# A scan feeding a two-layer network: one tile per weight load, and masks spread over the steps

## The chip, the cores and the metric

The kernel runs on one core of one Trainium2 chip. The metric is the time of one execution on the device in microseconds. The kernel before takes 139.41 us (median of three runs, 139.23 to 139.72). The profiled execution took 139.26 us, of which the profile covers a span of 137.5 us.

A core has five engines that run at the same time and wait for each other through semaphores: TensorE (PE, matrix products; PEld is its weight load), VectorE (DVE), ScalarE (ACT), GpSimd (POOL) and SyncE (SP, which here only issues transfers). Matrix products are written to PSUM, eight banks of 128 partitions by 512 fp32 values; the other operands lie in SBUF.

## The reference, cut to what matters

A recurrence with decay over the sequence (4 batches, 8 heads, 768 positions, 32 values and 16 states for each head), in chunks of 32, and then a network with a squared ReLU on the 3072 tokens:

```python
for c in range(nc):                       # chunks of the sequence
    cum = np.cumsum(la, axis=-1)          # la: log of the decays a
    L = np.exp(cum[:, :, :, None] - cum[:, :, None, :]) * causal
    CB = np.einsum('bhin,bhjn->bhij', Cc, Bc)
    y_intra = np.einsum('bhij,bhjd->bhid', CB * L, xc)
    y_inter = np.einsum('bhin,bhnd->bhid', Cc, state) * np.exp(cum)[..., None]
    y[:, :, sl] = y_intra + y_inter
    state = decay_full * state + sum_j(B_j x_j decay_from_j)
# [3072, 256] @ [256, 2048] -> relu, squared -> @ [2048, 256]
h = np.maximum(y_tokens @ w_in, 0.0)
out = h * h @ w_out
```

All inputs and the output are fp32.

## The kernel before

The work is cut into 12 units of 256 tokens (one batch, a third of the sequence). A unit has two chunks of 128 tokens; token `2t + r` of a unit lies at place t, half r. For each unit the kernel

- loads C, B and x, and scales C by the running product P of the decays and x by 1/P (`ph_prep`), so that no exponentials are needed,
- transposes C and B (`ph_tr`), on TensorE for units 0 to 3 and by the transfer engines after that,
- multiplies C and B into PSUM banks 0 to 3 (`ph_mt`) and masks the result into SBUF as bf16 (`ph_mask`, VectorE),
- adds up, in two other banks, y (masked products with x, and C with the state S), and the new state's sum U of both chunks (`ph_yu`), and copies y to `T`, which is what the network reads,
- makes S from U (`ph_s`): z = U + S before on VectorE, S = z times the decay on GpSimd, and a copy spread over the heads.

The network runs in steps of 256 hidden units, eight for each unit of tokens: `mm1` (four products into one bank, then ReLU on ScalarE), `square` on VectorE one step later, `mm2` four steps later. The work on the next units is hung into these steps. PSUM banks 4, 5 and 6 go round for `mm1`, y and U; bank 7 holds the output.

The loads of the weights, their casts to bf16, and the masks:

```python
BLOCKS = [(0, 2), (2, 4), (4, 8), (8, 12), (12, 16)]   # 128 hidden units each
w_in_b = wpool.tile([128, 2, 2048], BF16, name="w_in_b")
w_out_b = wpool.tile([128, 16, 256], BF16, name="w_out_b")
w_in_f = stage.tile([128, 2, 2048], FP32, name="w_in_f")
w_out_f = stage.tile([128, 16, 256], FP32, name="w_out_f")

def load_w(i, eng=None):
    f0, f1 = BLOCKS[i]
    (eng or nc.sync).dma_start(out=w_in_f[:, :, f0 * 128:f1 * 128], in_=...)
    (eng or nc.sync).dma_start(out=w_out_f[:, f0:f1, :], in_=...)

def cast_w(fp):
    f = 2 * fp
    f0, f1 = next(x for x in BLOCKS if x[0] <= f < x[1])
    nc.scalar.copy(out=_fap(w_in_b, f * 128, [[2048, 2], [128, 2], [1, 128]]),
                   in_=_fap(w_in_f, f0 * 128 + f - f0, [[2048, 2], [1, 2], [f1 - f0, 128]]))
    nc.gpsimd.tensor_copy(out=w_out_b[:, f:f + 2, :], in_=w_out_f[:, f:f + 2, :])

def ph_mask(k, q0, q1):        # banks q0 to q1 - 1
    nc.vector.tensor_tensor(out=live[k]["mts"][:, q0:q1]..., in0=pp[:, q0:q1, :],
                            in1=<the mask>, op=ALU.mult)
```

The order of the first part, and of the steps:

```python
ph_load(0, ...); load_w(0); load_w(1); ph_load(1)
load_w(2); load_w(3); ph_load(2); load_w(4); ph_load(3)
# ... decays, ph_prep and ph_tr of unit 0 ...
ph_mt(0)
ph_mask(0, 0, 1)
ph_yu(u=0)
ph_s(0, 0)
ph_s(0, 1)
for q in range(1, 4):
    ph_mask(0, q, q + 1)
cast_w(0)
cast_w(1)
ph_yu(y=0, late=True)          # y of unit 0, then the copy to T

for fp in range(2, 8):
    at(fp - 2, cast_w, fp)     # hung into steps 0 to 5
# unit 1: prep at step 1, ph_tr at 2, U and ph_mt at 3, ph_s and masks at 4 and 5, y at 7
# unit 2: prep at 4, ph_tr at 8, U and ph_mt at 9, ph_s and masks at 10 and 11
# unit 3: prep at 9, ph_tr at 10
for k in range(2, NU):         # from unit 2 on: the region of unit k
    s0 = 8 * k - 4
    at(s0, ph_yu, y=k, u=k + 1)
    at(s0, ph_mt, k + 1)
    for i in range(2):
        at(s0 + 1 + i, ph_s, k + 1, i)
        at(s0 + 1 + i, ph_mask, k + 1, 2 * i, 2 * i + 2)
```

Of the kernel before, what the change touches and what calls it, by code (L numbers as in the profile page):

```python
# [10 lines left out]
FP32 = mybir.dt.float32  # L11
BF16 = mybir.dt.bfloat16
AF = mybir.ActivationFunctionType
# [17 lines left out]
def kernel(  # L31
# [104 lines left out]
    def load_w(i, eng=None):  # L136
        f0, f1 = BLOCKS[i]
        (eng or nc.sync).dma_start(  # L138
            out=w_in_f[:, :, f0 * 128:f1 * 128],
            in_=_dap(moe_w_in, f0 * 128, [[2048, 128], [128 * 2048, 2], [1, (f1 - f0) * 128]]))  # L140
        (eng or nc.sync).dma_start(
            out=w_out_f[:, f0:f1, :],
            in_=moe_w_out[f0 * 128:f1 * 128, :].rearrange("(p f) d -> p f d", p=128))

    def cast_w(fp):
        f = 2 * fp
        f0, f1 = next(x for x in BLOCKS if x[0] <= f < x[1])
        nc.scalar.copy(out=_fap(w_in_b, f * 128, [[2048, 2], [128, 2], [1, 128]]),  # L148
                       in_=_fap(w_in_f, f0 * 128 + f - f0, [[2048, 2], [1, 2], [f1 - f0, 128]]))
        nc.gpsimd.tensor_copy(out=w_out_b[:, f:f + 2, :], in_=w_out_f[:, f:f + 2, :])  # L150

    live = {}

# [33 lines left out]
    def ph_tr(k):  # L187
        v = live.setdefault(k, {})
        bct = big.tile([128, 2, 3, 128], BF16, tag="bct", name=f"bct{k}")
        v["bct"] = bct  # L190
        if k >= NPE:
            nc.sync.dma_start_transpose(out=bct.rearrange("p r w t -> p (r w) t"),
                                        in_=jt[k % 3].rearrange("p r w t -> p (r w t)"))
            return
# [28 lines left out]
    def ph_yu(y=None, u=None, late=False):  # L223

        h = two_banks()
        begun = set()

        def mm(i, quads, dst, w, v, pos):
            need = [(i, q) for q in quads if (i, q) not in begun]
            begun.update(need)  # L230
            assert len(need) in (0, len(quads))
            nc.tensor.matmul(dst, w, v, start=bool(need), stop=False, skip_group_check=True,  # L232
                             **({} if pos is None else {"tile_position": pos}))

        def from_state():
            for i in range(2):
                S_i = live[y]["S"][i]
                if S_i is None:
                    continue
                for g in range(2):  # L240
                    mm(i, range(4), pp[:, h[i], g * 128:(g + 1) * 128], S_i[:, g * 128:(g + 1) * 128],
                       _fap(live[y]["bct"], 128 + g * 128 + i * 64, [[384, 2], [1, 64]]), None)

        if y is not None:
            v = live[y]
            if not late:
                from_state()
            for g in range(2):
                for r in range(2):
                    for i in range(2):  # L250
                        for q in range(4):
                            hd = 4 * g + q
                            mm(i, [q], pp[32 * q:32 * q + 32, h[i], g * 128:(g + 1) * 128],
                               v["xs"][64 * i:64 * i + 64, r, hd * 32:hd * 32 + 32],
                               v["mts"][64 * i:64 * i + 64, q, r, g, :], (64 * i, 32 * q))
# [11 lines left out]
        if y is not None:  # L267
            if late:
                from_state()
            T[y] = tpool.tile([128, 2, 2, 2, 64], BF16, tag="T", name=f"T{y}")  # L270
            nc.scalar.copy(out=_fap(T[y], 0, [[64, 2], [128, 4], [1, 64]]),  # L271
                           in_=_fap(pp, h[0] * 512, [[512, 2], [64, 4], [1, 64]]))
            live.pop(y)

    def ph_s(k, i):

        b, j = UNITS[k]
        v = live[k]
# [9 lines left out]
        if prev is None:  # L288
            nc.vector.tensor_scalar(out=S_c, in0=U, scalar1=ptot, scalar2=None, op0=ALU.mult)  # L289
        else:  # L290
            z = spool.tile([128, 64], FP32, tag="z", name=f"z{k}_{i}")
            nc.vector.tensor_tensor(out=z, in0=U, in1=prev, op=ALU.add)  # L292
            nc.gpsimd.tensor_scalar(out=S_c, in0=z, scalar1=ptot, scalar2=None, op0=ALU.mult)  # L293
        S_d = spool.tile([128, 256], BF16, tag=f"Sd{b}{i}", name=f"Sd{k}_{i}")
        nc.gpsimd.tensor_tensor(  # L295
            out=_fap(S_d, 0, [[128, 2], [32, 4], [1, 32]]), in0=_fap(S_c, 0, [[32, 2], [0, 4], [1, 32]]),
# [6 lines left out]
    def mm1(blk, fp):  # L303
        h = bank()
        for i in range(2):
            f = 2 * fp + i
            for g in range(2):
                nc.tensor.matmul(pp[:, h, i * 256:(i + 1) * 256], w_in_b[:, g, f * 128:(f + 1) * 128],  # L308
                                 T[blk][:, g].rearrange("p r u t -> p (r u t)"),
                                 start=(g == 0), stop=(g == 1), skip_group_check=True)  # L310
# [10 lines left out]
    def mm2(blk, fp):  # L321
        h2 = h2s.pop((blk, fp))
        for i in range(2):
            f = 2 * fp + i
            for r in range(2):
                nc.tensor.matmul(pp[:, 7, r * 256:(r + 1) * 256], h2[:, i, r * 128:(r + 1) * 128],  # L326
                                 w_out_b[:, f, :], start=(f == 0 and r == 0), stop=(f == 15),
                                 skip_group_check=True)
        if fp == 7:
            b, j = UNITS[blk]  # L330
# [4 lines left out]
    with tc.manual_schedule():  # L335
# [8 lines left out]
        ph_load(1)  # L344
        load_w(2)
        load_w(3)
        ph_load(2)
        load_w(4)
        ph_load(3)

        nc.vector.memset(zer, 0.0)
        nc.vector.memset(jt[0], 0.0)
        for i in range(1, 3):
            nc.gpsimd.memset(jt[i], 0.0)
        nc.vector.tensor_scalar(out=a_cl, in0=a_nat, scalar1=1e-6, scalar2=1.0, op0=ALU.max, op1=ALU.min)
        for u in range(2):
            nc.vector.tensor_tensor_scan(out=cp_r[:, u * 128:(u + 1) * 128], data0=a_cl[:, u * 128:(u + 1) * 128],
# [3 lines left out]
        for r in range(2):  # L361
            nc.tensor.transpose(ptr[:, r, :], _fap(cp_r, r, [[2, 128]]), eye_f)
        nc.scalar.copy(out=P_sb, in_=ptr)
        prep_b(0, nc.scalar)
        prep_c(0, nc.vector)
        nc.vector.reciprocal(out=_fap(Pinv, 0, [[96, 2], [3, 32]]), in_=_fap(P_sb, 0, [[96, 2], [3, 32]]))
# [4 lines left out]
        hp = bank()  # L371
        pps = pp[:, hp, 0:24].rearrange("p (u c) -> p u c", u=2)
# [12 lines left out]

        steps = [(b, f) for b in range(NU) for f in range(8)]
        todo = {}
# [11 lines left out]
        at(3, ph_mt, 1)  # L399
        at(4, ph_s, 1, 0)  # L400
        at(4, ph_s, 1, 1)
        at(4, ph_mask, 1, 0, 2)
        at(5, ph_mask, 1, 2, 4)
# [10 lines left out]
        for k in range(2, NU):  # L414
# [54 lines left out]
```

## Time and profile before

| engine | busy, us | share of the span | instructions |
|---|---|---|---|
| TensorE, products | 108.0 | 79% | 1572 |
| TensorE, weight loads | 89.3 | 65% | 1572 |
| VectorE | 84.0 | 61% | 158 |
| ScalarE | 78.7 | 57% | 133 |
| GpSimd | 55.3 | 40% | 104 |

The profile has several views. The page gives the busy share of each engine in 40 equal slices of the span, as digits in tenths. Its groups are instructions of one line, engine and operation: after the bar stand the busy time in us and the mean of one in ns, then how long the engine stood idle just before them, and what ended that wait. The timeline is in order of time: start, duration, engine, line, operation, output<-input, count, and in brackets the idle time before and its releaser. An engine with q behind its name is its instruction queue, which issues transfers; the duration there is the issue and not the transfer. The list of waits sums who waited for whom. The chain of waits goes back from the last instruction to what released it, step by step.

The chain of waits of the kernel before gives TensorE 61% of the span, VectorE and ScalarE 9% each, the queue that issues transfers 9% and the transfers 7%. The largest lines in it are the two products of the network, with 28% and 25%.

### The profile page before, as it was taken

Reading aid. Unit: us, or ns where it says so; the run is one execution under the profiler, and the core shown is the slowest. Engines: PE = TensorE matmul, PEld = TensorE weight load, DVE = VectorE, ACT = ScalarE, POOL = GpSimd, SP = SyncE. Lnnn points to the kernel's source line nnn. Section 1 sums busy time; section 2 is a strip of 40 time slices with the busy share of each in tenths; the row PEclk is TensorE's granted clock in tenths of the full one; section 3 lists DMA queues with packets and bytes.
Section 4 is the critical chain, followed back from the end, with each engine's and each line's share of the span. In section 5 each row is a group of like instructions: output and inputs, shape, how many; then the busy total and the mean of one; then the engine's idle time right before and its main releaser. Section 6 shows DMA issues by size and latency. Waiting matters only on the chain.

```text
span 137.5 us, 3855 instructions
## 1 busy us (share of the span) xinstructions
PE 108.0 (79%) x1572; PEld 89.3 (65%) x1572; DVE 84.0 (61%) x158; ACT 78.7 (57%) x133; POOL 55.3 (40%) x104
## 2 busy tenths in 40 slices
PE   0164000569999898998998989999999999999990
PEld 0141000437877786877887868888888878888770
DVE  1558000158799976869869778696786839534430
ACT  2200000997836567575675756767667676686640
POOL 4037190109966663916828349190542003000000
PEclk9999999999999999999999999999999999999999
DMA  5999999996001679539929599187902802010101
GB/s 93 235 303 205 368 243 303 214 150 131 0 5 51 127 120 114 94 82 141 150 90 90 111 120 164 58 97 146 119 19 89 49 2 81 2 76 5 76 0 76
DMA packets 48034, 15.81 MB, mean 115 GB/s; under 512 B 44240, under 2 KB 45072, under 8 KB 48016
## 3 DMA queue, kind: packets, MB, share of 16 engines
q1 hardware_dynamic: 46720, 15.18, 59.3%
q10 hardware_dynamic: 1296, 0.39, 1.7%
q8 instruction: 12, 0.20, 0.6%
q14 instruction: 6, 0.05, 0.1%
HBM read 10.84 MB, written 3.15 MB: 102 GB/s over the span
## 4 chain that ended last, share of the span: by engine, by line
PE 61%; DVE 9%; ACT 9%; SPq 9%; DMA 7%; issue 2%; ACTq 1%; DVEq 0%
PE pp L308 28%; PE pp L326 25%; SPq L130 7%; PE pp L232 6%; DVE mts L219 5%; DMA cb<-const_b 4%; ACT hb L312 3%; DMA w_in_f<-in_moe_w_in_dram 3%; ACT T L271 3%; ACT w_in_b L148 2%; DVE h L318 2%; PE pp L210 2%; DVE z L292 1%; ACT osb L332 1%; SPq L138 1%
## 5 line engine op out<-in xcount | busy, mean ns | idle before, releaser
L312 ACT ACTIVATE hb<-pp 128x512 bf16<-128x512 f32 x96 | 57.4, 598 | 29.7 <-PE pp L308 29.6
L308 PE MATMUL pp<-T,w_in_b 128*128 128x256 bf16 x384 | 60.0, 282 | 14.7 <-ACT T L271 12.4
L318 DVE TENSOR_TENSOR h<-hb 128x512 bf16<-128x512 bf16 x96 | 47.7, 515 | 33.5 <-ACT hb L312 32.6
L326 PE MATMUL pp<-w_out_b,h 128*128 128x256 bf16 x384 | 57.6, 275 | 0.3 <-ACT osb L332 0.3
L308 PEld LDWEIGHTS <-w_in_b 128*128 128x128 bf16 x384 | 37.4, 101 | 23.1 <-ACT w_in_b L148 11.6
L326 PEld LDWEIGHTS <-h 128*128 128x128 bf16 x384 | 37.9, 99 | 5.2 <-issue 0.5
L219 DVE TENSOR_TENSOR mts<-pp,cb 128x1024 bf16<-128x1024 f32 (+1 forms) x26 | 29.2, 1131 | 0.8 <-PE pp L210 0.8
L293 POOL TENSOR_SCALAR Sc<-z,Ptot 128x64 f32<-128x64 f32 x16 | 7.1, 443 | 35.5 <-DVE z L292 35.5
L148 ACT CAST w_in_b<-w_in_f 128x512 bf16<-128x512 f32 x8 | 7.8, 990 | 15.4 <-DMA w_in_f<-in_moe_w_in_dram 15.4
L295 POOL TENSOR_TENSOR Sd<-Sc,cb 128x256 bf16<-128x256 f32 x20 | 12.2, 612 | 10.2 <-DVE Sc L289 8.9
L174 POOL TENSOR_TENSOR xs<-x_nat,Pinv 128x512 bf16<-128x512 f32 x12 | 13.2, 1102 | 5.2 <-DMA x_nat<-in_x_dram 5.2
L157 POOL TENSOR_TENSOR jt<-C_nat,P_sb 128x128 bf16<-128x128 f32 x20 | 10.7, 554 | 0.0
L271 ACT CAST T<-pp 128x512 bf16<-128x512 f32 x12 | 7.0, 584 | 2.9 <-PE pp L232 2.6
L292 DVE TENSOR_TENSOR z<-pp,Sc 128x64 f32<-128x64 f32 x16 | 3.5, 221 | 7.7 <-ACT T L271 7.4
L150 POOL CAST w_out_b<-w_out_f 128x512 bf16<-128x512 f32 x8 | 4.8, 619 | 8.4 <-DMA w_out_f<-in_moe_w_out_dram 8.4
L232 PE MATMUL pp<-mts,xs 64*32 64x128 bf16 x384 | 6.2, 225 | 2.4 <-DVE mts L219 1.7
L332 ACT COPY osb<-pp 128x512 f32<-128x512 f32 x12 | 7.0, 581 | 1.6 <-PE pp L326 1.6
L169 POOL CAST jt<-B_nat 128x128 bf16<-128x128 f32 x22 | 7.2, 353 | 0.0
L232 PEld LDWEIGHTS <-xs 64*32 64x32 bf16 x384 | 3.5, 93 | 4.3 <-issue 3.2
L210 PE MATMUL pp<-bct 32*64 32x256 bf16 x192 | 5.6, 303 | 0.3 <-DVE bct L200 0.3
L232 PE MATMUL pp<-bct,Sd 128*128 128x128 bf16 x40 | 5.0, 223 | 0.5
L232 PE MATMUL pp<-xs,jt 64*32 64x64 bf16 x160 | 4.0, 203 | 1.3 <-ACT hb L312 1.1
(28 smaller groups left out, 27.3 us busy)
## 6 DMA issues: line engine op xcount, KB each, us to landing
x_nat<-in_x_dram SPq DMA_DIRECT2D x12, 256.0 KB, 4.7
out_dram<-osb SPq DMA_DIRECT2D x12, 256.0 KB, 3.9
C_nat<-in_C_dram SPq DMA_DIRECT2D x12, 128.0 KB, 4.1
w_in_f<-in_moe_w_in_dram SPq DMA_DIRECT2D x3, 512.0 KB, 5.4
w_out_f<-in_moe_w_out_dram SPq DMA_DIRECT2D x3, 512.0 KB, 6.1
B_nat<-in_B_dram SPq DMA_DIRECT2D x11, 128.0 KB, 4.3
w_in_f<-in_moe_w_in_dram SPq DMA_DIRECT2D x2, 256.0 KB, 5.6
w_out_f<-in_moe_w_out_dram SPq DMA_DIRECT2D x2, 256.0 KB, 5.6
```

The lines of the kernel that those rows point to most:

```text
L130: (eng or nc.sync).dma_start(out=dst, in_=_dap(src, (b * NH * S + j * 256) * w, [[2 * w, 128], [S * w, NH], [1, 2 * w]]))
L148: nc.scalar.copy(out=_fap(w_in_b, f * 128, [[2048, 2], [128, 2], [1, 128]]), in_=_fap(w_in_f, f0 * 128 + f - f0, [[2048, 2], [1, 2], [f1 - ...
L157: eng.tensor_tensor(out=_fap(jt[k % 3], 128 + 144 * g, [[384, 2], [32, 4], [1, 16]]), in0=_fap(loaded[k]["C"], 128 * g, [[16, 2], [32, 4], ...
L174: eng.tensor_tensor(out=_fap(xs, 0, [[256, 2], [32, 8], [1, 32]]), in0=_fap(loaded[k]["x"], 0, [[32, 2], [64, 8], [1, 32]]), in1=_fap(Pinv ...
L219: nc.vector.tensor_tensor(out=live[k]["mts"][:, q0:q1].rearrange("p q r g i -> p q (r g i)"), in0=pp[:, q0:q1, :], in1=_fap(cb, 128, [[0, ...
L232: nc.tensor.matmul(dst, w, v, start=bool(need), stop=False, skip_group_check=True, **({} if pos is None else {"tile_position": pos}))
L271: nc.scalar.copy(out=_fap(T[y], 0, [[64, 2], [128, 4], [1, 64]]), in_=_fap(pp, h[0] * 512, [[512, 2], [64, 4], [1, 64]]))
L295: nc.gpsimd.tensor_tensor(out=_fap(S_d, 0, [[128, 2], [32, 4], [1, 32]]), in0=_fap(S_c, 0, [[32, 2], [0, 4], [1, 32]]), in1=_fap(cb, 640, ...
L308: nc.tensor.matmul(pp[:, h, i * 256:(i + 1) * 256], w_in_b[:, g, f * 128:(f + 1) * 128], T[blk][:, g].rearrange("p r u t -> p (r u t)"), s ...
L312: nc.scalar.activation(out=hb.rearrange("p i t -> p (i t)"), in_=pp[:, h, :], func=AF.Relu)
L318: nc.vector.tensor_tensor(out=h2, in0=hb, in1=hb, op=ALU.mult)
L326: nc.tensor.matmul(pp[:, 7, r * 256:(r + 1) * 256], h2[:, i, r * 128:(r + 1) * 128], w_out_b[:, f, :], start=(f == 0 and r == 0), stop=(f ...
```

## The change

It has six parts:

- Each of the five weight loads gets a tile of its own (`w_in_f`, `w_out_f`), and each cast too (`w_in_b`, `w_out_b`), so that a reader depends only on the load that it reads. The hidden units are dealt out in pairs within each cast, so a cast reads every second element of w_in in all blocks. The fifth load is issued ahead of units 2 and 3.
- The masks of later units go bank by bank, one in every second step, and both chunks' `ph_s` come before the first of them.
- In the region of a unit, the products for the new state U stand ahead of those of the masked y.
- The first unit is spread over the engines: its transposed C and B leave PSUM by VectorE and ScalarE, half each; ScalarE copies the fourth bank of products, and GpSimd masks it; ScalarE makes the state spread over the heads out of U directly; T is copied by ScalarE and VectorE, half each.
- Idle products: products of a tile of zeros into an unused part of bank 7, 32, 8, 5, 24 and 5 of them at five places of the first part. They are meant to keep TensorE at work while it waits.
- The masks of unit 1 go one bank at a time too, in the same two steps.

```diff
+    NIDLE = (32, 8, 5, 24, 5)
...
-    w_in_b = wpool.tile([128, 2, 2048], BF16, name="w_in_b")
-    w_out_b = wpool.tile([128, 16, 256], BF16, name="w_out_b")
-    w_in_f = stage.tile([128, 2, 2048], FP32, name="w_in_f")
-    w_out_f = stage.tile([128, 16, 256], FP32, name="w_out_f")
+    idle = const.tile([128, 128], BF16, name="idle")
+    w_in_b = [wpool.tile([128, 2, 2, 128], BF16, name=f"w_in_b{i}") for i in range(8)]
+    w_out_b = [wpool.tile([128, 2, 256], BF16, name=f"w_out_b{i}") for i in range(8)]
+    w_in_f = [stage.tile([128, 2, (f1 - f0) * 128], FP32, name=f"w_in_f{i}") for i, (f0, f1) in enumerate(BLOCKS)]
+    w_out_f = [stage.tile([128, f1 - f0, 256], FP32, name=f"w_out_f{i}") for i, (f0, f1) in enumerate(BLOCKS)]
...
+        dst = w_in_b[fp]
+        src = _fap(w_in_f[i], o * 128, [[n, 2], [1, 2], [2, 128]])
...
+    def idle_products(n):
+        for _ in range(n):
+            nc.tensor.matmul(pp[:, 7, 256:384], idle, idle, start=True, stop=True, skip_group_check=True)
...
             v = live[y]
             if not late:
                 from_state()
-            <32 products of the masked y>
         if u is not None:
             <products of U>
         if y is not None:
+            <32 products of the masked y>
...
+            if y == 0:
+                for i, fn in enumerate((nc.scalar.copy, nc.vector.tensor_copy)):
+                    fn(out=_fap(T[y], i * 64, [[128, 4], [1, 64]]),
+                       in_=_fap(pp, h[i] * 512, [[64, 4], [1, 64]]))
+                return
...
         load_w(3)
+        load_w(4)
         ph_load(2)
-        load_w(4)
         ph_load(3)
...
+        idle_products(NIDLE[2])
         ph_mt(0)
+        sc3 = big.tile([128, 512], BF16, tag="sc3", name="sc3")
+        nc.scalar.copy(out=sc3, in_=pp[:, 3, :])
         ph_mask(0, 0, 1)
+        turn[0] = 6
         ph_yu(u=0)
-        ph_s(0, 0)
+        b0 = live[0]["h"]
+        for q in range(4):
+            p = slice(32 * q, 32 * q + 32)
+            nc.scalar.activation(out=_fap(S_00[p], 32 * q, [[128, 2], [1, 32]]),
+                                 in_=_fap(pp[p], b0[0] * 512 + 256, [[32, 2], [1, 32]]),
+                                 func=AF.Copy, scale=Ptot[p, 0, 0:1])
+        nc.gpsimd.tensor_tensor(out=live[0]["mts"][:, 3].rearrange("p r g i -> p (r g i)"), in0=sc3,
+                                in1=_fap(cb, 128, [[1, 512]]), op=ALU.mult)
+        idle_products(NIDLE[3])
+        ph_mask(0, 1, 2)
+        ph_mask(0, 2, 3)
+        ph_s(0, 0, S_00)
         ph_s(0, 1)
-        for q in range(1, 4):
-            ph_mask(0, q, q + 1)
         cast_w(0)
+        ph_yu(y=0, late=True)
+        idle_products(NIDLE[4])
         cast_w(1)
-        ph_yu(y=0, late=True)
...
             for i in range(2):
-                at(s0 + 1 + i, ph_s, k + 1, i)
-                at(s0 + 1 + i, ph_mask, k + 1, 2 * i, 2 * i + 2)
+                at(s0 + 1, ph_s, k + 1, i)
+            for q in range(4):
+                at(s0 + 1 + 2 * q, ph_mask, k + 1, q, q + 1)
```

More of the change, by code (lines that the diff above doesn't have):

```diff
@@ L138, in load_w, with cast_w @@
         (eng or nc.sync).dma_start(
-            out=w_in_f[:, :, f0 * 128:f1 * 128],
+            out=w_in_f[i],
             in_=_dap(moe_w_in, f0 * 128, [[2048, 128], [128 * 2048, 2], [1, (f1 - f0) * 128]]))
         (eng or nc.sync).dma_start(
[L142 to L150, printed above, removed]
+            out=w_out_f[i],
+            in_=_dap(moe_w_out, f0 * 128 * 256, [[512, 128], [256 * 256, (f1 - f0) // 2], [1, 512]]))
+    def cast_w(fp, eng=None):
+        i = next(i for i, x in enumerate(BLOCKS) if x[0] <= 2 * fp < x[1])
+        f0, f1 = BLOCKS[i]
+        o, n = 2 * fp - f0, (f1 - f0) * 128
+        dst = w_in_b[fp]
+        src = _fap(w_in_f[i], o * 128, [[n, 2], [1, 2], [2, 128]])
+        if eng is nc.vector:
+            eng.tensor_copy(out=dst, in_=src)
+        else:
+            nc.scalar.copy(out=dst, in_=src)
+        nc.gpsimd.tensor_copy(out=w_out_b[fp], in_=w_out_f[i][:, o:o + 2, :])
+    def idle_products(n):
+        for _ in range(n):
+            nc.tensor.matmul(pp[:, 7, 256:384], idle, idle, start=True, stop=True, skip_group_check=True)
     live = {}
@@ L193, in ph_tr @@
                                         in_=jt[k % 3].rearrange("p r w t -> p (r w t)"))
+            return
+        if k == 0:
+            for r in range(2):
+                tr = pp[:, 6 + r, 0:192].bitcast(BF16)
+                for w in range(3):
+                    nc.tensor.transpose(tr[:, w * 128:(w + 1) * 128], jt[0][:, r, w, :], eye_b)
+                o = bct[:, r].rearrange("p w t -> p (w t)")
+                if r == 0:
+                    nc.vector.tensor_copy(out=o, in_=tr)
+                else:
+                    nc.scalar.copy(out=o, in_=tr)
             return
@@ L247, in ph_yu @@
                 from_state()
[L248 to L255, printed above, removed]
         if u is not None:
@@ L267, in ph_yu @@
         if y is not None:
+            v = live[y]
+            for g in range(2):
+                for r in range(2):
+                    for i in range(2):
+                        for q in range(4):
+                            hd = 4 * g + q
+                            mm(i, [q], pp[32 * q:32 * q + 32, h[i], g * 128:(g + 1) * 128],
+                               v["xs"][64 * i:64 * i + 64, r, hd * 32:hd * 32 + 32],
+                               v["mts"][64 * i:64 * i + 64, q, r, g, :], (64 * i, 32 * q))
+        if y is not None:
             if late:
@@ L270, in ph_yu, with ph_s @@
             T[y] = tpool.tile([128, 2, 2, 2, 64], BF16, tag="T", name=f"T{y}")
+            live.pop(y)
+            if y == 0:
+                for i, fn in enumerate((nc.scalar.copy, nc.vector.tensor_copy)):
+                    fn(out=_fap(T[y], i * 64, [[128, 4], [1, 64]]),
+                       in_=_fap(pp, h[i] * 512, [[64, 4], [1, 64]]))
+                return
             nc.scalar.copy(out=_fap(T[y], 0, [[64, 2], [128, 4], [1, 64]]),
                            in_=_fap(pp, h[0] * 512, [[512, 2], [64, 4], [1, 64]]))
[L273 to L275 removed]
+    def ph_s(k, i, S_d=None):
         b, j = UNITS[k]
@@ L293, in ph_s @@
             nc.gpsimd.tensor_scalar(out=S_c, in0=z, scalar1=ptot, scalar2=None, op0=ALU.mult)
+        if S_d is not None:
+            state[b] = (S_c, S_d)
+            v["S"].append(S_d)
+            return
         S_d = spool.tile([128, 256], BF16, tag=f"Sd{b}{i}", name=f"Sd{k}_{i}")
@@ L307, in mm1 @@
             for g in range(2):
-                nc.tensor.matmul(pp[:, h, i * 256:(i + 1) * 256], w_in_b[:, g, f * 128:(f + 1) * 128],
+                nc.tensor.matmul(pp[:, h, i * 256:(i + 1) * 256], w_in_b[fp][:, g, i, :],
                                  T[blk][:, g].rearrange("p r u t -> p (r u t)"),
@@ L326, in mm2 @@
                 nc.tensor.matmul(pp[:, 7, r * 256:(r + 1) * 256], h2[:, i, r * 128:(r + 1) * 128],
-                                 w_out_b[:, f, :], start=(f == 0 and r == 0), stop=(f == 15),
+                                 w_out_b[fp][:, i, :], start=(f == 0 and r == 0), stop=(f == 15),
                                  skip_group_check=True)
@@ L346 @@
         load_w(3)
+        load_w(4)
         ph_load(2)
-        load_w(4)
         ph_load(3)
+        nc.vector.memset(idle, 0.0)
         nc.vector.memset(zer, 0.0)
         nc.vector.memset(jt[0], 0.0)
+        S_00 = spool.tile([128, 256], BF16, tag="Sd00", name="Sd0_0")
+        nc.gpsimd.memset(S_00, 0.0)
         for i in range(1, 3):
             nc.gpsimd.memset(jt[i], 0.0)
+        idle_products(NIDLE[0])
         nc.vector.tensor_scalar(out=a_cl, in0=a_nat, scalar1=1e-6, scalar2=1.0, op0=ALU.max, op1=ALU.min)
@@ L363 @@
         nc.scalar.copy(out=P_sb, in_=ptr)
+        idle_products(NIDLE[1])
         prep_b(0, nc.scalar)
@@ L370 @@
         ph_tr(0)
-        hp = bank()
-        pps = pp[:, hp, 0:24].rearrange("p (u c) -> p u c", u=2)
+        pps = pp[:, hp, 256:280].rearrange("p (u c) -> p u c", u=2)
         nc.tensor.matmul(pps, spread, pick_p, start=True, stop=True)
         nc.scalar.copy(out=Ptot, in_=pps)
+        idle_products(NIDLE[2])
         ph_mt(0)
+        sc3 = big.tile([128, 512], BF16, tag="sc3", name="sc3")
+        nc.scalar.copy(out=sc3, in_=pp[:, 3, :])
         ph_mask(0, 0, 1)
+        turn[0] = 6
         ph_yu(u=0)
-        ph_s(0, 0)
+        b0 = live[0]["h"]
[10 more added lines that the diff above has]
+        ph_s(0, 0, S_00)
         ph_s(0, 1)
-        for q in range(1, 4):
-            ph_mask(0, q, q + 1)
         cast_w(0)
+        ph_yu(y=0, late=True)
+        idle_products(NIDLE[4])
         cast_w(1)
-        ph_yu(y=0, late=True)
         steps = [(b, f) for b in range(NU) for f in range(8)]
@@ L401 @@
         at(4, ph_s, 1, 1)
-        at(4, ph_mask, 1, 0, 2)
-        at(5, ph_mask, 1, 2, 4)
+        for q in range(4):
+            at(4 + q // 2, ph_mask, 1, q, q + 1)
         at(5, nc.vector.reciprocal, out=_fap(Pinv, 1, [[96, 2], [3, 32], [1, 2]]),
@@ L421 @@
             for i in range(2):
-                at(s0 + 1 + i, ph_s, k + 1, i)
-                at(s0 + 1 + i, ph_mask, k + 1, 2 * i, 2 * i + 2)
+                at(s0 + 1, ph_s, k + 1, i)
+            for q in range(4):
+                at(s0 + 1 + 2 * q, ph_mask, k + 1, q, q + 1)
         for k in range(2, NU):
```

## The prediction

> **What bounds the kernel now.** I read the page first, for where the engines stand idle, then the chain of work that ended last, then the timeline of the stretches that the two pointed to. Row by row of 3.44 us, the page has this:
>
> ```profile
> PE   0164000569999898998998989999999999999990
> DVE  1558000158799976869869778696786839534430
> ACT  2200000997836567575675756767667676686640
> DMA  5999999996001679539929599187902802010101
> L308 PE MATMUL pp<-T,w_in_b 128*128 128x256 bf16 x384 | 60.0, 282 | 14.7 <-ACT T L271 12.4
> L148 ACT CAST w_in_b<-w_in_f 128x512 bf16<-128x512 f32 x8 | 7.8, 990 | 15.4 <-DMA w_in_f<-in_moe_w_in_dram 15.4
> ```
>
> From about 13 to 25 us TensorE, VectorE and ScalarE do nothing while the transfers run at full share. After that TensorE is busy to the end. So there are two regimes: a head that ends when the first feed-forward product may start, and a body in which TensorE sets the pace. ScalarE's first cast of w_in waited 15.4 us for a load of w_in. The timeline says which load:
>
> ```profile
> 18.23 1.06 POOL L174 TENSOR_TENSOR xs<-x_nat,Pinv 128x512 bf16<-128x512 f32 x1
> 19.07 0.58 SPq L138 DMA_DIRECT2D w_in_f<-in_moe_w_in_dram  x1
> 23.72 1.18 ACT L148 CAST w_in_b<-w_in_f 128x512 bf16<-128x512 f32 x2 [15.41 <-DMA w_in_f<-in_moe_w_in_dram]
> 24.81 0.57 ACT L271 CAST T<-pp 128x512 bf16<-128x512 f32 x1
> 25.28 1.11 ACT L148 CAST w_in_b<-w_in_f 128x512 bf16<-128x512 f32 x1
> 25.43 0.80 PE L308 MATMUL pp<-T,w_in_b 128*128 128x256 bf16 x3 [12.35 <-ACT T L271]
> ```
>
> The cast of hidden units 0 to 255 starts just after the fifth load of w_in (issued at 19.07) has landed, though its own load was issued at 2.27 and had an issue-to-landing time like the others (median 5.6 us): all loads write one tile, and each slice of w_in_f spans both halves of the tile, so the wait is for the whole. T, whose PSUM was ready at 13.1 (the last small products ran at 12.68 for 0.40), stands behind that cast in ScalarE's order. The w_out casts on GpSimd show the honest landings, since w_out's slices don't interleave:
>
> ```profile
> 11.71 1.23 POOL L150 CAST w_out_b<-w_out_f 128x512 bf16<-128x512 f32 x2
> 16.63 1.17 POOL L150 CAST w_out_b<-w_out_f 128x512 bf16<-128x512 f32 x2 [3.68 <-DMA w_out_f<-in_moe_w_out_dram]
> 17.74 0.53 POOL L169 CAST jt<-B_nat 128x128 bf16<-128x128 f32 x2
> 19.47 1.17 POOL L150 CAST w_out_b<-w_out_f 128x512 bf16<-128x512 f32 x2 [0.17 <-DMA w_out_f<-in_moe_w_out_dram]
> 25.20 0.61 POOL L150 CAST w_out_b<-w_out_f 128x512 bf16<-128x512 f32 x1 [4.57 <-DMA w_out_f<-in_moe_w_out_dram]
> ```
>
> Block 2 is there at 16.6, block 3 at 19.5, block 4 at 25.2. In the body, a step is 0.87 us (0.44 for the first product's four matmuls, 0.44 for the second's), and units 3 to 7 show one stall each:
>
> ```profile
> 63.96 1.21 DVE L219 TENSOR_TENSOR mts<-pp,cb 128x1024 bf16<-128x1024 f32 x1
> 64.09 0.60 PE L308 MATMUL pp<-T,w_in_b 128*128 128x256 bf16 x4 [0.45 <-DVE z L292]
> ```
>
> The feed-forward product needs a PSUM bank that still holds the state U of the second chunk; VectorE reads it (z) only after a 1.2 us mask. The idle times of this kind in the list of waits sum to 2.3 us over 5 places.
>
> [...] four products with w_out took 1.06 us at 32.60 and 0.60 at 35.32, after which steps of 0.44 are the rule; the throttle row (all 9) doesn't show it. [...] T waited behind a cast on ScalarE, and B of unit 1 behind the 16.63 cast on GpSimd. [...]
>
> **The change, part by part.**
>
> (1) A tile per weight load. The cast of block 0 now waits for block 0 alone (issued 2.27, landing by about 8). The reading step of the cast is now always two elements; before, blocks of two casts were read with a step of 2 (1.18 for two, 0.6 each) and those of four with a step of 4 (1.10 each). So six casts fall from 1.1 to 0.6 us, 3 us of ScalarE, in steps where ScalarE took 1.5 us each.
>
> (2) The first unit. VectorE had four masks after the products of C and B (0.69 + 1.88) with the state (0.28 + 0.23) between. Now VectorE does three (9.1 to 11.0), ScalarE copies the fourth bank (0.6) and GpSimd multiplies it (about 1.06, from the 128x512 product), ending near 10.8; ScalarE builds the decayed state itself. So y's products run near 11.0, and T (two halves on two engines) is ready near 12.1 instead of 13.7. The first product starts there: 13.3 us earlier than 25.43. Most of this is not kept, as the following shows.
>
> (3) What ends the wait next. ScalarE's order is cast 1, cast 2, relu 0, cast 3, relu 1, cast 4, relu 2. Block 2 of w_in lands at about 15.3 (issued 9.84, latency 5.5), so relu 0 comes near 16.5 and relu 1 near 17.7. GpSimd's order is w_out 0, 1, 2, 3, then B and x of unit 1: as before, 16.63 is set by block 2 of w_out, so B of unit 1 is done near 18.3 and x at 19.3. TensorE, in order, has the transposes of unit 1 ahead of step 2's product, hence it idles from about 13.0 to 18.3 whatever the first unit gained. After 5.3 us of idling its clock is probably low again, so the idle products warm it for nothing. From there: transposes (0.85 as at 27.09) to 19.15, step 2's product to 20.0, relu 2 to 20.7, which frees the banks that U of unit 1 needs. In the trace of before the same place is 30.11, and relu 6, the first one after all casts, starts 5.47 us later (34.98 + 0.60 = 35.58). 20.7 + 5.5 = 26.2; the shorter casts help little, as TensorE at half rate needs 1.7 us for a step anyway. Block 4 is now queued before unit 2 instead of behind it: 1 MB after 19.5 at about 400 GB/s lands near 22, and its cast is wanted near 23. Gain of the head: 35.58 - 26.2 = 9.4, say 9.3 us.
>
> (4) Units 2 and 3 load after block 4. Together the same bytes have landed at about 28 (x of unit 3: issued 21.54, up to 6.6 us). Then unit 2 is complete near 25.5, and its preparation (0.96 + 0.52 + 1.06 on GpSimd) ends near 26.6 to 28; its transposes come in step 8, near 27.6, and need only the first two, so at most some tenths are lost.
>
> (5) Masks bank by bank and both z first. z of both chunks now come ahead of all masks: z at 62.16, GpSimd's S (0.44), the second z near 63.0 instead of 63.83, so that the bank is free before TensorE wants it (about 63.5). 5 places of 0.45 to 0.51 go: 2.3 us. Four masks of about 0.65 cost 0.2 us more than two of 1.21, on a VectorE that is 6.8 of 9 us busy: nothing. The last mask now ends less than a step ahead of y, which is why U's products go in front of y's; I give no gain for that order.
>
> (6) Idle products. 74 in all; at half rate 128 columns take about 0.11 us (the six transposes: 0.80), so 32 take 3.4 us from 1.2, before the scan's result at 4.96; the 24 end by 12 at the worst. Nothing on the path.
>
> Sum: 139.41 - 9.3 - 2.3 = 127.8 us. The clock may stay high through the gap (half a chance, worth 1 to 1.5 us): 127.2.
>
> **Rivals.** (a) Nothing else holds the head: TensorE goes on from 12.1 without a stop. Then 13 of the head and 2.3 go, and 124 us is left, less with a warm clock. Against it stand the landings at 16.6 and 19.5, which this change doesn't hasten. (b) The loads become the bound: block 4 and then units 2 and 3 come later than TensorE wants them, steps 4 to 10 stall by 2 to 3 us, and the time is 130 to 131. For it: transfers are at full share until 27 us in any case. (c) The finer masks pile up: squares come late, y waits for the fourth mask in each unit; 0.3 us for each of 9 units gives 130. Against: VectorE idles in every unit. (d) The false wait was hidden, and nothing changes: the empty TensorE slices speak against it.
>
> **Range and chances.** The head's gain is 7.5 to 13 us, and the body's -0.5 to 3: 80% between 123.8 and 130.6. A change within 2% would need four fifths of the 11.6 us to be lost. Faster 0.96, same 0.03, slower 0.01.
>
> **What would show it.** The first cast of w_in near 10.6 and the first product near 12; then a TensorE gap to about 18 ended by GpSimd's B of unit 1 (or relu behind a cast that waits for block 2); relu 6 near 26; no wait of the feed-forward product for z after the second unit; four matmuls at 1.06 us around 19 to 23 if the clock fell. It is wrong if TensorE runs on from 12, if steps 4 to 10 wait for loads of units 2 or 3, or if waits of y for a mask appear in each unit.

## The result and the profile after

The changed kernel takes 127.22 us (median of four runs, 126.32 to 128.94). The ratio to the kernel before is 0.909, with a 95% interval of 0.903 to 0.915. The profiled span went from 137.5 to 125.7 us. Here and below, the ratios and their intervals leave out executions more than 1.5% above the fastest of their kernel, and the medians do not; of the trace of the run by_need, which is of such an execution, only the order of its waits is read.

From the page of the changed kernel, TensorE's row of busy tenths (3.14 us each here), the granted clock, and the group of the w_in casts:

```profile
PE   6776308999899999999999999999999999999980
PEclk9999955599999999999999999999999999999998
L156 ACT CAST w_in_b<-w_in_f 128x512 bf16<-128x512 f32 x8 | 5.2, 645 | 3.6 <-DMA w_in_f<-in_moe_w_in_dram 3.6
```

The 15.4 us of waiting for w_in are 3.6 now, and a cast takes 0.65 us on average instead of 0.99. TensorE still has a hole, at 13 to 19 us, and the clock row stands at 5 from 15.7 to 25.1 us, in the hole and behind it. The timeline of the changed kernel says what ends the hole and what follows:

```profile
10.59 0.64 ACT L156 CAST w_in_b<-w_in_f 128x512 bf16<-128x512 f32 x1
...
12.49 1.03 PE L341 MATMUL pp<-T,w_in_b 128*128 128x256 bf16 x8 [0.33 <-DVE T L298]
...
12.88 0.47 SPq L140 DMA_DIRECT2D w_in_f<-in_moe_w_in_dram  x1
...
17.11 1.24 POOL L157 CAST w_out_b<-w_out_f 128x512 bf16<-128x512 f32 x2 [3.41 <-DMA w_out_f<-in_moe_w_out_dram]
...
18.29 0.53 POOL L180 CAST jt<-B_nat 128x128 bf16<-128x128 f32 x2
...
18.88 0.82 PE L221 MATMUL pp<-cb,jt 128*128 128x128 bf16 x6 [5.35 <-POOL jt L180]
...
19.50 1.06 PE L341 MATMUL pp<-T,w_in_b 128*128 128x256 bf16 x4
...
26.67 0.60 ACT L345 ACTIVATE hb<-pp 128x512 bf16<-128x512 f32 x1 [0.35 <-PE pp L341]
```

The first cast of w_in runs at 10.59, before the fifth load is even issued (12.88): the wait for all five loads is gone. The first feed-forward product runs at 12.49 instead of 25.43, and two steps later TensorE stands 5.35 us until GpSimd has B of unit 1, which came behind the cast that waited for block 2 of w_out. Four products then take 1.06 us. The last line is the relu of step 6, the second one behind the last cast: 26.67 against 35.58 before.

In the body, the kernel before has this in its list of TensorE's waits (us in total, times, the longest):

```profile
PE pp L308 <- DVE z L292: 2.3, 5, 0.5
```

With the change no wait for z is left in that list from 28 us on. The region of unit 3, again from the timeline:

```profile
43.76 0.23 DVE L321 TENSOR_TENSOR z<-pp,Sc 128x64 f32<-128x64 f32 x1 [0.70 <-ACT T L301]
...
44.56 0.23 DVE L321 TENSOR_TENSOR z<-pp,Sc 128x64 f32<-128x64 f32 x1 [0.58 <-POOL Sc L322]
...
44.70 0.68 DVE L241 TENSOR_TENSOR mts<-pp,cb 128x512 bf16<-128x512 f32 x1
...
45.06 0.60 PE L341 MATMUL pp<-T,w_in_b 128*128 128x256 bf16 x4
```

Both z are done before the first mask, and the product at 45.06 has no wait. The copies to T are a good ruler for the body, one for each unit. From unit 2's to unit 7's the five distances were 8.67, 9.15, 8.79, 9.07 and 8.72 us; now they are 8.17, 8.47, 8.18, 8.47 and 8.13. From there on they are the same to within 0.03 us (8.41 and 8.41, 8.08 and 8.11).

So of the 11.8 us that the span lost, 8.9 lie ahead of the relu of step 6 and 2.9 behind it.

### The profile page after: what moved, and what is told of

It is laid out like the page before. It is cut to its first block, busy times and chain, and to the rows that moved or that the text cites. A ratio compares the mean times of both kernels' runs of the same rounds, so it can differ in the third digit from the quotient of the medians.

```text
span 125.7 us, 4026 instructions
## 1 busy us (share of the span) xinstructions
PE 110.9 (88%) x1646; PEld 93.2 (74%) x1646; DVE 84.9 (68%) x179; ACT 78.3 (62%) x139; POOL 57.7 (46%) x105
## 4 chain that ended last, share of the span: by engine, by line
PE 75%; DMA 10%; ACT 4%; DVE 3%; SPq 3%; POOL 1%; issue 1%; ACTq 1%; DVEq 0%
PE pp L341 34%; PE pp L359 31%; PE pp L254 6%; DMA w_out_f<-in_moe_w_out_dram 6%; DMA cb<-const_b 4%; PE pp L232 3%; ACT hb L345 3%; SPq L132 2%; DVE mts L241 2%; POOL w_out_b L157 1%; ACT osb L365 1%; PE pp L221 1%; DVE h L351 1%; SPq L140 0%; ACTq L132 0%
## 5 line engine op out<-in xcount | busy, mean ns | idle before, releaser
L351 DVE TENSOR_TENSOR h<-hb 128x512 bf16<-128x512 bf16 x96 | 48.4, 516 | 16.5 <-ACT hb L345 15.8
L341 PE MATMUL pp<-T,w_in_b 128*128 128x256 bf16 x384 | 59.2, 279 | 0.3 <-DVE T L298 0.3
L241 DVE TENSOR_TENSOR mts<-pp,cb 128x512 bf16<-128x512 f32 (+1 forms) x45 | 31.3, 704 | 1.2 <-PE pp L232 1.2
L328 POOL TENSOR_TENSOR Sd<-Sc,cb 128x256 bf16<-128x256 f32 x19 | 13.4, 705 | 1.9 <-DVE Sc L318 0.6
L168 POOL TENSOR_TENSOR jt<-C_nat,P_sb 128x128 bf16<-128x128 f32 x20 | 9.4, 490 | 0.0
L161 PE MATMUL pp<-idle 128*128 128x128 bf16 x74 | 6.6, 260 | 1.3 <-DVE idle L384 1.0
L156 ACT CAST w_in_b<-w_in_f 128x512 bf16<-128x512 f32 x8 | 5.2, 645 | 3.6 <-DMA w_in_f<-in_moe_w_in_dram 3.6
L161 PEld LDWEIGHTS <-idle 128*128 128x128 bf16 x74 | 6.0, 121 | 1.5 <-DVE idle L384 1.0
L221 PE MATMUL pp<-cb,jt 128*128 128x128 bf16 x18 | 1.8, 249 | 5.4 <-POOL jt L180 5.4
L221 PEld LDWEIGHTS <-jt 128*128 128x128 bf16 x18 | 1.4, 111 | 5.7 <-POOL jt L180 5.6
```

Source lines behind the costliest of these rows:

```text
L161: nc.tensor.matmul(pp[:, 7, 256:384], idle, idle, start=True, stop=True, skip_group_check=True)
L168: eng.tensor_tensor(out=_fap(jt[k % 3], 128 + 144 * g, [[384, 2], [32, 4], [1, 16]]), in0=_fap(loaded[k]["C"], 128 * g, [[16, 2], [32, 4], ...
L241: nc.vector.tensor_tensor(out=live[k]["mts"][:, q0:q1].rearrange("p q r g i -> p q (r g i)"), in0=pp[:, q0:q1, :], in1=_fap(cb, 128, [[0, ...
L328: nc.gpsimd.tensor_tensor(out=_fap(S_d, 0, [[128, 2], [32, 4], [1, 32]]), in0=_fap(S_c, 0, [[32, 2], [0, 4], [1, 32]]), in1=_fap(cb, 640, ...
L341: nc.tensor.matmul(pp[:, h, i * 256:(i + 1) * 256], w_in_b[fp][:, g, i, :], T[blk][:, g].rearrange("p r u t -> p (r u t)"), start=(g == 0) ...
L351: nc.vector.tensor_tensor(out=h2, in0=hb, in1=hb, op=ALU.mult)
```

## Experiments

All ratios are to the kernel before, run on the same chip.

**The weight tiles alone.** The kernel before with the new tiles, pairs and load order, and nothing else:

```diff
-    w_in_f = stage.tile([128, 2, 2048], FP32, name="w_in_f")
+    w_in_f = [stage.tile([128, 2, (f1 - f0) * 128], FP32, name=f"w_in_f{i}") for i, (f0, f1) in enumerate(BLOCKS)]
     (w_out_f, w_in_b and w_out_b alike)
-        ph_load(2); load_w(4)
+        load_w(4); ph_load(2)
```

> The kernel before with the weight loads alone changed: a tile per load and per cast, the pairs, the fifth load ahead of units 2 and 3. No idle products, first unit and masks as before. Theory: the head is set by GpSimd's order behind block 2 of w_out (landing near 17), whatever the first unit does, so nearly the whole gain of the head (8.5 to 9.3 us, relu of step 6 near 26.5 to 27) is here, and the five stalls of the body stay: 130 to 131 us. Rival 1: the spread first unit and the idle products carry part of the head: 132 or more. Rival 2: the false wait gave little by itself: over 135.

129.8 us, ratio 0.930 (0.925 to 0.935). From its list of waits of TensorE after 8 us:

```profile
PE pp L204 <- POOL jt L174: 2.8, 1, 2.8
PE pp L313 <- DVE z L297: 2.4, 5, 0.6
```

The five waits for z are still there, and the head's hole ends in the same place, with GpSimd's B of unit 1. The hole is 2.8 us long instead of 5.35 only because the first product starts later. The relu of step 6 comes at 26.28, as early as with the whole change. Both rivals fall. The ruler by T stays at 44.52 us from unit 2 to unit 7 (44.40 before), so all of this gain lies in the head.

The run changes three things at once: the tiles, the step of the casts, and the place of the fifth load. Their shares were not tried. For the last there is an estimate from the trace of the whole change: the fifth load of w_in was issued at 12.88 there and took 8.2 us to land, so a wait for all five would have ended near 21.1 instead of 23.7. The order of the loads alone would be worth about 2.6 us.

**Masks and states alone.** The kernel before with the masks bank by bank, both states first, and U ahead of the masked y:

```diff
             for i in range(2):
-                at(s0 + 1 + i, ph_s, k + 1, i)
-                at(s0 + 1 + i, ph_mask, k + 1, 2 * i, 2 * i + 2)
+                at(s0 + 1, ph_s, k + 1, i)
+            for q in range(4):
+                at(s0 + 1 + 2 * q, ph_mask, k + 1, q, q + 1)
```

> The kernel before with the masks bank by bank, both states first, and U ahead of the masked y; loads as before. Theory: the five waits of the feed-forward product for z (2.3 us) go and some tenths more by the shorter region, the head stays at 25.4: 136.3 to 137.3 us. Rival: the head's late loads or VectorE's longer masks take it back: 138.5 to 139.5.

136.4 us, ratio 0.977 (0.972 to 0.982). In its list of TensorE's waits no wait for z is left, and the first product still waits for T, 13.1 us against 12.4 before:

```profile
PE pp L309 <- ACT T L272: 13.1, 1, 13.1
```

The ruler by T is 41.27 us, as short as with the whole change (41.42). With the two parts the whole is accounted for: 9.7 us for the first and 3.2 for the second, by medians, against 12.3 for the change; the 0.6 us too many are within the intervals.

**Without the idle products; without the spread first unit.** The changed kernel with the five counts set to zero, and the changed kernel with the first unit's masks, copies and state on the old engines:

```diff
-    NIDLE = (32, 8, 5, 24, 5)
+    NIDLE = (0, 0, 0, 0, 0)
```

> The changed kernel without its 74 idle products. Theory: they warm a clock that falls again in the gap from 13.5 to 18.9, and their only effect, a somewhat earlier first product, is hidden behind GpSimd: within 0.5 us of the changed kernel (127.2), relu of step 6 near 26.7. Rival: they keep the clock high where it counts: 129 or more.

> The changed kernel with the first unit on its old engines (four masks on VectorE, one T copy, one copy of C and B), idle products kept. Theory: the first feed-forward product starts 1 to 1.5 us later (near 13.7), but the next gap still ends with GpSimd's B of unit 1 near 18.3 to 18.9: within 0.5 us of 127.2. Rival: the 1.5 us are paid in full: 128.7.

126.7 us (0.905, 0.899 to 0.911) and 126.4 us (0.906, 0.902 to 0.911). Neither part carries any of the gain. Without the spread, T is copied at 13.80 and the hole is 3.1 us, ended by the same cast of B.

**Filling the hole.** 80 idle products more, at step 2:

```diff
+        at(2, idle_products, 80)
         at(2, ph_tr, 1)
```

> The changed kernel with 80 more idle products at step 2, in the gap ahead of unit 1's transposes. They take some 4.7 us at full clock and end near 18.2, before GpSimd's B of unit 1. Theory: the clock fell because TensorE stood idle; kept at work, the products after the gap run at full rate (0.44 instead of 1.06 us for four), relu of step 6 comes 1.5 to 2.5 us earlier, 125 to 126 us. Rival: between 19 and 26 us ScalarE's casts and the landings set the pace and the low clock is hidden: 127, with products at 0.44.

126.1 us, ratio 0.904 (0.902 to 0.907): the interval overlaps that of the change (0.903 to 0.915), so by the times alone the gain isn't sure. The timeline of TensorE has the mechanism:

```profile
13.94 4.63 PE L161 MATMUL pp<-idle 128*128 128x128 bf16 x80
18.59 0.51 PE L221 MATMUL pp<-cb,jt 128*128 128x128 bf16 x6
18.93 0.60 PE L341 MATMUL pp<-T,w_in_b 128*128 128x256 bf16 x4
...
26.91 0.51 PE L221 MATMUL pp<-cb,jt 128*128 128x128 bf16 x6 [0.88 <-POOL jt L180]
```

The same four products take 0.60 us here and 1.06 behind the 5.35 us hole of the change, so idling did lower the clock there. The relu of step 6 starts near 24.0 (two relus from 23.47 take 1.08), 2.7 us earlier. But unit 2's transposes then wait 0.88 us for GpSimd, and at unit 2's region (32.15 against 33.40) only 1.25 us are left of the 2.7. This says that something other than the clock holds the head, and the next runs ask for it.

**GpSimd's queue** (pool_first). The casts of w_out from step 2 on go behind the preparation of unit 1:

```diff
+        for fp in range(2, 8):
+            at(max(fp - 2, 1), cast_out, fp)     # after prep_b(1), prep_x(1)
```

> The changed kernel with GpSimd's casts of w_out for steps 2 and later put behind the preparation of unit 1 (B, x). Theory: the transposes of unit 1 then run near 14.5 instead of 18.9; the gap's next end is relu 2, behind cast 4 of w_in on ScalarE (landing 18.4), near 19.6 instead of 20.6: 1 to 1.5 us less, 125.5 to 126.2. Rival: ScalarE and the loads hold the head anyway: 127.

125.8 us, ratio 0.901 (0.899 to 0.903; this just touches the interval of the change). The transposes of unit 1 run at 15.06 instead of 18.88; then TensorE waits 0.93 and 1.46 us for relus, which stand behind casts of w_in on ScalarE. After these waits four products take 1.06 us again, from 20.83 on.

**Both queues** (both_first). In addition, the relus of steps 0 and 1 go ahead of the casts that wait for block 2, and 20 idle products stand at step 2:

```diff
+            for fp in post.pop(s, []):           # after mm1 of step s
+                cast_w(fp, split=True)           # w_in only
```

> As pool_first, and on ScalarE the relus of steps 0 and 1 ahead of the casts that wait for block 2, each later cast behind the relu of an earlier step; 20 idle products at step 2. Theory: with both FIFO waits gone, step 2 starts when w_in's block 2 is cast (near 16.4), step 4 with block 3 (near 19.1), step 6 with block 4 (near 22.5): relu of step 6 near 23 instead of 26.7. Then units 2 and 3, whose loads land near 26.7 and 28.5, hold steps 8 to 12 by some 2 us: 124.5 to 126. Rival: no gain from the order of the queues: 127.

126.0 us, ratio 0.903 (0.899 to 0.906), no better than GpSimd's queue alone, though the relu of step 6 comes at 23.04, 3.6 us earlier than with the change. Its timeline, first of TensorE, then of GpSimd:

```profile
24.36 0.28 PE L260 MATMUL pp<-bct,Sd 128*128 128x128 bf16 x2 [1.15 <-POOL Sd L334]
...
27.10 0.51 PE L227 MATMUL pp<-cb,jt 128*128 128x128 bf16 x6 [1.13 <-POOL jt L186]
```

```profile
22.94 0.61 POOL L150 CAST w_out_b<-w_out_f 128x512 bf16<-128x512 f32 x1 [1.37 <-DMA w_out_f<-in_moe_w_out_dram]
23.52 0.78 POOL L334 TENSOR_TENSOR Sd<-Sc,cb 128x256 bf16<-128x256 f32 x1
...
25.80 0.78 POOL L174 TENSOR_TENSOR jt<-C_nat,P_sb 128x128 bf16<-128x128 f32 x2
```

The saving was given back two steps later, to the same kind of wait one block on. GpSimd's cast waits until 22.94 for block 4 of w_out, which is not wanted before step 10, and S of unit 1 and C of unit 2 stand behind it. The run that filled the hole and the one with GpSimd's queue alone have this cast at 22.51 and 22.45, and all three reach unit 2's region 9.3 to 9.6 us after it. That would explain why three different gains at step 6 ended within 0.4 us of each other; the next run tries it.

**Block 4 behind unit 2 on GpSimd** (gp_order; to the kernel with both queues in order):

```diff
+            if k == 2:                           # after ph_prep(2)
+                at(4, cast_out, 6)
+                at(5, cast_out, 7)
```

> As both_first, with GpSimd's casts of block 4 of w_out behind the preparation of unit 2. In both_first the relu of step 6 came at 23.0 instead of 26.7, but y of unit 1 then waited 1.1 us for GpSimd's S and unit 2's transposes 1.1 us for its B, both behind the cast that waits for block 4 of w_out (landing 22.9). Theory: the first of these waits goes, and the second shrinks to what the loads of unit 2 (queued behind block 4) allow: step 12's region near 31.3 instead of 32.3, 124.8 to 125.5. Rival: the loads of unit 2 hold it just as long: 126.

125.5 us, ratio 0.897 (0.892 to 0.901), below the interval of the change; it overlaps that of both queues in order. The wait for S is gone, and unit 2's region comes at 31.16, 1.2 us earlier than with both queues in order (32.34). So the place of that cast did hold this stretch. What is left are waits for GpSimd of 0.43 us at unit 2's transposes and 0.85 at unit 3's; GpSimd itself had waited 0.37 and 0.27 us for the loads of unit 2.

**Loads in the order of need** (by_need; to gp_order). All of w_in, block 2 of w_out, unit 2, the rest of w_out, unit 3; unit 3's preparation and transposes one step later:

```diff
-        load_w(2)
-        load_w(3)
-        load_w(4)
+        for i in (2, 3, 4):
+            load_w(i, what="i")
+        load_w(2, what="o")
         ph_load(2)
+        load_w(3, what="o")
+        load_w(4, what="o")
         ph_load(3)
```

> As gp_order, and the loads in the order of need: all of w_in, block 2 of w_out, unit 2, blocks 3 and 4 of w_out, unit 3; unit 3's preparation and transposes one step later, GpSimd's w_out casts behind what is wanted sooner. Theory: the head is now bound by the order in which the transfers land; with unit 2 landing near 23.5 its transposes don't wait, and only unit 3 (landing near 28.5) holds step 12, whose region comes near 29.5 to 30.5: 122.5 to 124.5, the fastest. Rival: the transfers as a whole bind, and any order only shifts the wait: 125.5 to 126.

127.3 us, ratio 0.909 (0.905 to 0.913), slower than gp_order and outside the 122.5 to 124.5 us expected. From the timeline of GpSimd:

```profile
26.29 2.67 POOL L152 CAST w_out_b<-w_out_f 128x512 bf16<-128x512 f32 x4
...
30.85 0.78 POOL L176 TENSOR_TENSOR jt<-C_nat,P_sb 128x128 bf16<-128x128 f32 x2
```

None of these waited for a transfer: once block 2 of w_out has landed (20.84), GpSimd works without a break. Four casts, the state of unit 2 and the preparation of unit 3 stand in one queue, and unit 3's transposes wait for it. The late landing of w_out's blocks had bunched the casts. That GpSimd's own work is the bound here is argued from this one trace and was not tried by taking casts off it.

**U ahead of y; the size of the masks.** The changed kernel with the masked y's products first again, and the changed kernel with two masks of two banks again, but both states still ahead of them:

```diff
-            for q in range(4):
-                at(s0 + 1 + 2 * q, ph_mask, k + 1, q, q + 1)
+            for i in range(2):
+                at(s0 + 1 + i, ph_mask, k + 1, 2 * i, 2 * i + 2)
```

> The changed kernel with the masked y's products ahead of U's again. Theory: the fourth mask ends nearly a step ahead of the region, so nothing or at most 0.1 us per region is lost: 127.2 to 128.2. Rival: y waits for the fourth mask in each region, 0.3 us or more for nine: 130 or more.

> The changed kernel with the masks in pairs of banks again (two of 1.2 us, in the first and second step after the region), but both states still ahead of them. Theory: the gain of the body is the bank that is free earlier, not the fine masks: no wait of the feed-forward product for z, regions 8.1 to 8.5 us apart as with the change, 126.5 to 127.5. Rival: a 1.2 us mask behind z makes the squares late or holds ScalarE's relu: a wait of TensorE in each unit comes back, 128.5 to 130.

With y first, 127.0 us and a ratio of 0.911 (0.908 to 0.915), and the ruler by T is 41.30 us against 41.42: the order of the region's products is worth nothing that can be seen. With the masks in pairs, 129.0 us and 0.917 (0.912 to 0.923). The median lies in the rival's range, but the ratio stands for 128.3 us, between the two ranges, and its interval overlaps that of the change. So I read the ruler as well: from unit 2's copy to unit 7's it is 44.40 us before, 41.42 with the change and 42.57 here. Putting the states first gives 1.8 of the 3.0 us, the finer masks the other 1.2. The timeline shows how:

```profile
45.34 1.21 DVE L241 TENSOR_TENSOR mts<-pp,cb 128x1024 bf16<-128x1024 f32 x1
...
46.48 2.95 DVE L351 TENSOR_TENSOR h<-hb 128x512 bf16<-128x512 bf16 x6
...
48.15 0.61 PE L359 MATMUL pp<-w_out_b,h 128*128 128x256 bf16 x4 [0.16 <-DVE h L351]
48.19 0.60 ACT L345 ACTIVATE hb<-pp 128x512 bf16<-128x512 f32 x1 [0.48 <-DVE h L351]
```

Six squares stand one after the other behind the second mask, and two steps later both TensorE and ScalarE wait for one of them. My theory held for the wait for z and fell for the masks: the late squares of the rival are real. By the ruler they cost 0.3 to 0.4 us in each of the last four of the five distances (8.84, 8.49, 8.77 and 8.44 us), and nothing in the first (8.03).

**What is enough.** The queue orders of gp_order, with the first unit on its old engines and no idle products at all:

> The orders of gp_order (125.5), with the first unit on its old engines and without any idle products: tiles per load, masks and states as changed, and the queues of ScalarE and GpSimd in the order of need. Theory: the loads hold the head, so neither the spread first unit nor the idle products are worth anything even here, though the first product comes near 13.8 instead of 12.9: 125 to 126.2. Rival: with the gap at TensorE shorter, the later first product or a low clock is now paid: 127 or more.

125.3 us (124.91 to 125.61), ratio 0.896 (0.892 to 0.899): the lowest median of all, clear of the change but not of gp_order. Its first product runs at 13.83, and four products take 1.03 to 1.06 us until about 22.8. Neither shows in the time, and unit 2's region comes at 30.96, against 31.16 in gp_order.

## Why the prediction was right, step by step

- **(1) Tiles.** Right. The fifth load no longer holds the first cast (10.59, for 10.6 predicted), and the six casts fell to about 0.65 us. The run with the tiles alone shows 9.7 of the 12.3 us.
- **(2) The first unit.** The first product was 0.4 us later than worked out (12.49 for 12.1). That most of it would not be kept was right: without the spread nothing was lost, so none of it was kept.
- **(3) What ends the wait next.** The mechanism was right to the instruction: GpSimd's B of unit 1, behind block 2 of w_out. The size was off by 0.5 us, since that block landed at 17.1 and not at 16.6. The relu of step 6 came at 26.67 for 26.2, and the head gained 8.9 us for 9.3. The clock fell as thought likely, which was an estimate of mine: behind the hole four products took 1.06 us and followed each other in 0.85 (23.73, 24.58, 25.43), the 1.7 us a step that the prediction took. The 0.6 us credited to the half chance that it would not fall were not there. The 1 to 1.5 us that a high clock was said to be worth agree with the run that filled the hole: 1.25 us at unit 2's region. The prediction calls relu 6 the first one after all casts; the first is that of step 5 (34.98 before, 25.73 with the change). The reading of 35.58 stands.
- **(4) Units 2 and 3.** Right for the change: unit 2's transposes at 28.29 waited for nothing. With it, block 4 of w_out was there at 22.58, for "near 22", and the transfers moved 394 GB/s from 15.7 to 18.8 us, for the 400 taken. In the experiments that hastened step 6, the cast of block 4, and unit 2 behind it on GpSimd, became the bound at once.
- **(5) The body.** 3.0 us for 2.3; this term was mis-sized. I summed the idle times of TensorE in the list of waits. There four products are drawn with 0.60 us, but they follow each other in 0.44 (117.44, 117.88, 118.31 with the change), so each listed wait leaves out 0.16 us of what it costs. Five of them are 0.8 us, and 2.3 and 0.8 make the 3.0 measured but for 0.1. "Four masks cost nothing" was wrong in the sign: with pairs of banks, late squares take back 1.2 of the 3.0 us, and the finer masks avoid that. Giving the order of U and y no gain was right.
- **(6) Idle products.** Right: nothing on the path, and no gain either.

That the median (127.22) hits the predicted 127.2 is luck. By the terms the gain was 0.4 us less in the head, 0.6 more in the body and 0.6 less for the clock, which makes 127.6 us; the rest is within the spread of the executions. A change within 2% would have needed three quarters of the gain to be lost (8.8 of 11.6 us), not four fifths.

Rivals (a), (c) and (d) fell. Of (c) one wait is left: in unit 2's region, whose masks still go in pairs, y waits 0.50 us for one. (b) did not happen in the change. That the loads hold the fastest kernels is not shown: the run with the loads in the order of need was slower, and gp_order waits for both GpSimd and loads.

## What to carry to other kernels

When a large tile is filled by several transfers, ask which regions they span in the tile, not which bytes they write: here the slices interleaved, and the first reader waited 15.4 us, until the last load, issued at 19.07, had landed. After that wait was gone, the next one was found by following the order of the work on the engines that convert the data. A cast for much later that waited for its load held what stood behind it: with both queues in order, the cast of block 4 waited 1.37 us on GpSimd, and TensorE then waited 1.15 us for S of unit 1. So casts belong at the place where they are wanted, not where they could first run. Four of them bunched together took 2.67 us in by_need and held unit 3's transposes as well. And work that makes an early stage faster, or keeps TensorE busy through a wait, should be tried only once the wait behind that stage has been found: here the idle products and the spread first unit gained nothing (126.7 and 126.4 us without them, 127.2 with both).

## What the runs showed of the hardware

In the leanest kernel the row of the granted clock and the durations of the products don't agree. From its page and its timeline:

```profile
PEclk9999999999999999999999999999999999999997
```

```profile
21.13 1.06 PE L349 MATMUL pp<-w_out_b,h 128*128 128x256 bf16 x4
...
23.73 0.60 PE L349 MATMUL pp<-w_out_b,h 128*128 128x256 bf16 x4
```

The row shows 9 where four products took 1.06 us. In all runs of the kernels without idle products (the kernel before, the tiles alone, the masks and states alone, no_idle and lean) the mean granted clock was 0.994 to 1.000, though in the kernel before and in lean four products took 1.06 us for a stretch. In the four runs of the changed kernel it was 0.933 to 0.955, and its row falls to 5. Why the row differs was not shown. The readings here rest on the durations of the products.

In the changed kernel the 32 idle products from 0.97 on took 3.59 us, or 0.11 each, and the 24 from 8.79 on took 1.51, or 0.06 each. In the kernel before, whose first feed-forward product ran at 25.43, four of them took 1.06 us until about 34.6 and 0.60 after that; in the leanest, where the first ran at 13.83, they took 1.03 to 1.06 us until about 22.8. Both are some 9 us, with waits in between.

Behind the holes of the changed kernel (5.35 us) and of the kernel with masks in pairs (3.71 us) four products took 1.06 us; behind the two waits of 1.15 and 1.13 us with both queues in order they took 0.60. In the kernel with GpSimd's queue alone no wait after the first product was longer than 1.46 us, and four products took 1.06 us again:

```profile
16.12 0.61 PE L347 MATMUL pp<-T,w_in_b 128*128 128x256 bf16 x4 [0.55 <-ACT w_in_b L161]
...
19.33 0.24 PE L260 MATMUL pp<-xs,jt 64*32 64x64 bf16 x12 [1.46 <-ACT hb L351]
...
20.83 1.06 PE L365 MATMUL pp<-w_out_b,h 128*128 128x256 bf16 x4
```

From 15.57 to 19.33 TensorE was busy for 0.82 of 3.76 us there, or 22%. With both queues in order it was busy for 2.22 of the 3.40 us from 22.60 to 26.00, or 65%, around the first of its two waits. The two runs differ in the busy share of such a stretch and a little in the longest wait; whether either of the two lowered the clock was not tried.
